# One core, attention into a gated convolution: a new hand-written order of 637 operations, with some query loads ahead of key and value loads

## The chip, the cores and the metric

One core of a Trainium2 chip runs the whole program. The metric is the device time of one execution in microseconds (us); the median over several runs of the same program is compared. The engines are TensorE (PE, with its weight loader PEld), VectorE (DVE), ScalarE (ACT), GpSimd (POOL) and SyncE (SP); POOL and SP do little here but issue DMA transfers.

## What is computed

A linear attention without softmax, normalised per head, feeds a feed-forward part with a convolution over the sequence and a gate:

```python
kv = einsum('bhsd,bhse->bhde', k, v)                # 8 batches, 8 heads, 576 rows, 64 wide
o = einsum('bhsd,bhde->bhse', q, kv)
o = o / sqrt(mean(o * o, axis=-1) + 1e-06) * g_norm
x = o.transpose(0, 2, 1, 3).reshape(8, 576, 512)
h = maximum(x @ w_in, 0)                            # 512 -> 1024
c = conv_w[0] * h[s-1] + conv_w[1] * h[s] + conv_w[2] * h[s+1]
out = (h * sigmoid(c)) @ w_out                      # 1024 -> 512
```

The inputs and the output are float32; the matrix products run in bfloat16 with float32 sums.

## The kernel before

The program is a list of 852 short tokens, the string `ORDER`. Each token names a small function, its arguments and, behind an `@`, the buffers that it takes; a loop at the end of the kernel calls the functions in the list's order. After that each instruction is tied to the one before it on its engine, so that the list alone sets the order of work on every engine; nothing is rescheduled. Semaphores hold an instruction back until its data and its buffer are there.

```python
for token in ORDER.split():
    what, _, at = token.partition("@")
    slots[:] = [int(s) for s in at.split(",")] if at else []
    name, *args = what.split(".")
    ops[name](*(int(a) if a.isdigit() else a for a in args))
```

The first argument of most tokens is the batch (0 to 7). Two batches share one buffer of `h` (a pair, 0 to 3), and there are two such buffers. PSUM is one tile `banks` of eight banks; `@2` means bank 2, or banks 2 and 3 where an operation takes two. The tokens that matter below, with the line under which the profile lists them:

- `Lq`, `Lk`, `Lv` (L347): POOL issues the load of q, k or v of one batch, with a cast to bfloat16. There are three buffers of q and two each of k and v, so a load waits until the last reader of the batch before it in the same buffer is through.
- `kv` (L402), `kz` (L479): k times v of a batch, 72 matmuls of 64 by 64 on quarters of the array. `kva` and `kvd` copy the result to `kvb` on ACT (L416) or DVE (L414). `kx` (L489, SP) copies `kvb` with its halves exchanged.
- `qt` (L433): transposes half of a batch's q on the PE; `qd` (L443, DVE) copies it out. Batches 6 and 7 use `tq` (L467, a transposing DMA on SP) instead.
- `ot` (L460), `ox` (L500): q times kv for a quarter of a batch, four matmuls on quarters of the array (64 by 64).
- Batches 2 and 3 are normalised in one way: `sq` (L509, ACT) squares, `on` (L528, PE) sums, `nl` (L545, ACT) takes the reciprocal root, `mo` (L556, DVE) writes the normalised `x`.
- Batches 4 to 7 go in pairs: `sq` and `oc` (L521, ACT, a copy), then `ss` (L566, PE, 16 matmuls on 32 columns), `ln` (L574, ACT), `sl` (L581 to L584, DVE, four steps), `sp` (L593, PE, two matmuls on 32 rows of the array that spread the factors), and `mu` (L599, DVE), which multiplies a quarter of `x`.
- `hk` (L658), `hs` (L628), `hm` (L613): `x @ w_in` for one of eight blocks `f` of 128 columns of `w_in`, over a half (`hk`, `hs`) or all (`hm`) of the rows of a batch. These use the full array. `hm` needs all four quarters of `x`. `rh` (L640) and `re` (L619) apply the maximum on ACT.
- The convolution and the gate are mostly on DVE: `ta` (L681, L682: two scaled copies), `aa` (L687), `ab` (L692), then `sg` (L698, sigmoid on ACT), then `mg` (L722, the product). They share two buffers `taps`.
- `om` (L732): four of the eight matmuls of `h @ w_out` for 128 rows of the output, on the full array; `ea` (L738, ACT) or `ed` (L743, DVE) copies the row block out of PSUM into one of six buffers `row`, and `st` (L748, SP) stores it. The last row block can be done in two halves of 256 columns: `oh` (L757), `eh` on ACT (L767) or `dh` on DVE (L772), `sh` (L777).

So the PE takes turns between three kinds of work: matmuls on the full array (`hk`, `hs`, `hm`, `on`, `om`), on quarters (`kv`, `kz`, `qt`, `ot`, `ox`), and on strips of 32 rows or columns (`sp`, `ss`). Below, a *run* is a stretch of PE work that is not on the full array, between two stretches that are.

Of the kernel before, what the change touches and what calls it, by code (L numbers as in the profile page):

```python
# [82 lines left out]
mo.2.0.1@2 om.0.3.0.4@4 ea.0.2@1 ot.2.1.1@6 ot.2.1.0@2 mg.1.1.0 om.0.3.4.4 ed.0.3@2 sq.2.1.0@1 sq.2.1.1@2 on.2.1.0@0
nl.2.1.0@9 mo.2.1.0 om.0.0.0.4@5 hk.1.3.0.0@4 on.2.1.1@0 st.0.2 nl.2.1.1@0 mo.2.1.1 om.0.0.4.4 ed.0.0@3 ot.2.0.0@2
sq.2.0.0@3 hk.1.3.0.1 rh.1.3.0 st.0.0 kv.3.0.2@0 kvd.3.0.2@0 on.2.0.0@6 nl.2.0.0@1 mo.2.0.0 hs.2.0.1@4 rh.2.0.1@1
hs.2.5.1@5 rh.2.5.1 ot.3.1.1@0 sq.3.1.1@4 ta.1.1.5@1 ot.3.0.1@6 sq.3.0.1@5 hs.2.1.1@4 rh.2.1.1 hs.2.4.0@5 rh.2.4.0
ta.1.1.4 ta.1.1.2@0 pn hs.2.4.1@2 rh.2.4.1 hs.2.1.0@3 rh.2.1.0 on.3.1.1@4 nl.3.1.1@2 hs.2.2.0@2 rh.2.2.0 hs.2.5.0@3
rh.2.5.0 on.3.0.1@4 nl.3.0.1@3 aa.1.1.2 mo.3.1.1@0 hs.2.2.1@2 rh.2.2.1 hs.2.0.0@3 rh.2.0.0 ot.3.0.0@0 sq.3.0.0@6
mo.3.0.1 qt.4.0.0@4 qd.4.0.0@3 ta.1.1.3 ab.1.1.2 aa.1.1.1 ot.3.1.0@2 sq.3.1.0@7 hs.2.3.1@6 rh.2.3.1 on.3.0.0@4
nl.3.0.0@4 hs.3.4.1@7 rh.3.4.1 hs.3.1.1@6 rh.3.1.1 on.3.1.0@4 nl.3.1.0@5 mo.3.0.0 hs.3.6.1@7 rh.3.6.1 hs.2.6.0@6  # L90
mo.3.1.0 qt.5.0.0@4 qd.5.0.0@0 ab.1.1.1 qt.4.1.0@0 qd.4.1.0@4 sg.1.1.5 sg.1.1.4 Lq.6.0.4@0 mg.1.1.2 ta.1.1.6@1
ta.1.1.7 aa.1.1.3 hs.2.3.0@7 rh.2.3.0 hs.3.0.1@2 rh.3.0.1 rh.2.6.0 sg.1.1.3 sg.1.1.2 hs.3.7.0@3 hs.3.2.0@4 rh.3.2.0
hs.3.3.0@5 rh.3.3.0 rh.3.7.0 kv.4.0.2@0 kvd.4.0.2@1 hs.3.0.0@2 hs.3.3.1@6 mg.1.1.1 Lk.5.0.4@0 rh.3.3.1 hs.3.2.1@7
rh.3.2.1 hs.3.7.1@4 rh.3.7.1 hs.3.6.0@5 rh.3.6.0 rh.3.0.0 ab.1.1.3 ta.2.2.2@0 ta.2.2.3 hs.3.4.0@3 rh.3.4.0 sg.1.1.7
hs.3.1.0@4 hs.3.5.0@5 sg.1.1.6 rh.3.1.0 qt.5.1.0@0 qd.5.1.0@2 ot.4.0.0@6 sq.4.0.0@0 mg.1.1.3 rh.3.5.0 om.0.7.0.4@2
Lv.5.0.4@1 Lq.7.0.4@1 Lk.6.0.4@1 oc.4.0.0@6 hs.2.7.1@3 rh.2.7.1 ot.4.0.1@0 sq.4.0.1@1 oc.4.0.1@7 kv.5.0.2@4 ta.2.2.0@1
kvd.5.0.2@2 ot.4.1.0@6 oc.4.1.0@8 om.0.7.4.4 aa.2.2.1 ta.2.2.1 ed.0.7@4 aa.2.2.0 ot.5.0.0@4 sq.4.1.0@2 sq.5.0.0@3
# [727 lines left out]
```

## Time and profile before

| | us |
|---|---|
| median of 3 runs (lowest to highest) | 177.68 (177.53 to 177.69) |
| span of the profiled execution, first to last instruction | 175.6 |
| PE busy | 167.9 |
| DVE busy | 149.5 |
| ACT busy | 148.9 |
| POOL busy | 22.2 |

The profiled execution's own time is not listed apart from its span; the median of the runs is 2.1 us above the span. "Busy" counts an instruction from its start to its end, so engines whose instructions overlap (PE above all) look busier than they are: on the PE the distance from one start to the next tells more than the length of a matmul. A releaser behind "<-" is what ended an idle stretch; "issue" means that the profile shows nothing that was waited for. The view by stretches has, for each engine, its busy time and in brackets its instructions, then the granted PE clock and the load on the DMA engines.

### The profile page before, as it was taken

How to read it: one execution, taken by the hardware profiler on the slowest of the kernel's cores; microseconds unless marked ns; L12 is line 12 of the kernel's file. 1: busy time of each engine (PE TensorE's matmuls, PEld its weight loads, DVE VectorE, ACT ScalarE, POOL GpSimd, SP SyncE). 2: the span in 40 equal slices, each digit the busy share in tenths (PEclk: the TensorE clock that was granted, in tenths of full speed). 3: DMA queues.
4: the chain of work that ended last, by engine and by line, in shares of the span. 5: the costliest groups of instructions: out<-in, count | busy, mean ns of one | idle time of the engine just before them, and what ended most of it. 6: DMA issues, size and time to landing. Idle time of an engine off the chain costs nothing.

```text
span 175.6 us, 5070 instructions
## 1 busy us (share of the span) xinstructions
PE 167.9 (96%) x2097; PEld 100.0 (57%) x2114; DVE 149.5 (85%) x290; ACT 148.9 (85%) x268; POOL 22.2 (13%) x35
## 2 busy tenths in 40 slices
PE   7979999999999999999999999999999999999992
PEld 2334766676447677644467764444877744444451
DVE  2796638899688899999999998989999999999950
ACT  2368899999978999999999998999999967676721
POOL 3094512200603013030000000000000000000000
PEclk9999999999999999999999999999999999999999
DMA  5999999999999999999999050330310003064486
GB/s 159 392 323 207 207 207 207 208 208 209 207 241 230 227 207 207 170 182 197 258 181 161 14 134 0 119 123 0 119 63 0 0 0 116 13 239 175 179 304 237
DMA packets 25911, 29.11 MB, mean 166 GB/s; under 512 B 6036, under 2 KB 20384, under 8 KB 25888
## 3 DMA queue, kind: packets, MB, share of 16 engines
q0 software_dynamic: 13296, 14.50, 49.2%
q1 hardware_dynamic: 12048, 13.11, 26.2%
q10 hardware_dynamic: 544, 1.18, 1.7%
q8 instruction: 16, 0.26, 0.6%
q14 instruction: 7, 0.06, 0.1%
HBM read 32.52 MB, written 9.44 MB: 239 GB/s over the span
## 4 chain that ended last, share of the span: by engine, by line
PE 76%; DVE 12%; ACT 5%; DMA 3%; issue 3%; ACTq 0%; DVEq 0%
PE banks L732 32%; PE banks L628 14%; PE banks L613 9%; PE banks L658 4%; DMA stg<-in_v_dram 3%; PE banks L460 3%; DVE h L722 2%; PE banks L708 2%; ACT taps L698 2%; PE banks L402 2%; PE banks L593 2%; PE banks L433 1%; PE banks L528 1%; DVE taps L681 1%; PE banks L286 1%
## 5 line engine op out<-in xcount | busy, mean ns | idle before, releaser
L732 PE MATMUL banks<-w_out_sb,h 128*128 128x512 bf16 x267 | 62.8, 379 | 1.2 <-issue 0.6
L698 ACT ACTIVATE taps<-taps,cw 128x576 bf16<-128x576 bf16 (+1 forms) x44 | 40.6, 958 | 5.7 <-DVE taps L692 5.5
L732 PEld LDWEIGHTS <-h 128*128 128x128 bf16 x280 | 26.2, 98 | 30.0 <-issue 1.1
L628 PE MATMUL banks<-x,w_in_sb 128*128 128x288 bf16 (+2 forms) x256 | 34.2, 286 | 0.0
L640 ACT ACTIVATE h<-banks 128x288 bf16<-128x288 f32 (+2 forms) x80 | 29.5, 460 | 0.3 <-PE banks L658 0.2
L628 PEld LDWEIGHTS <-w_in_sb 128*128 128x128 bf16 x256 | 24.4, 98 | 7.8 <-issue 0.8
L722 DVE TENSOR_TENSOR h<-h,taps 128x1152 bf16<-128x1152 bf16 (+1 forms) x24 | 22.8, 952 | 1.2 <-ACT taps L698 1.2
L687 DVE TENSOR_TENSOR taps<-taps 128x1152 bf16<-128x1152 bf16 (+1 forms) x22 | 21.5, 978 | 0.5
L509 ACT ACTIVATE sq<-banks 128x576 bf16<-128x576 f32 (+2 forms) x32 | 20.8, 691 | 1.1 <-PE banks L460 1.1
L692 DVE TENSOR_TENSOR taps<-taps,h 128x1152 bf16<-128x1152 bf16 (+1 forms) x22 | 21.4, 972 | 0.3
L681 DVE TENSOR_SCALAR taps<-h,cw 128x576 bf16<-128x576 bf16 (+1 forms) x44 | 18.7, 424 | 0.6 <-ACT h L665 0.5
L682 DVE TENSOR_SCALAR taps<-h,cw 128x576 bf16<-128x576 bf16 (+1 forms) x44 | 18.4, 418 | 0.0
L738 ACT ACTIVATE row<-banks 128x512 f32<-128x512 f32 x23 | 13.5, 597 | 5.7 <-PE banks L732 4.2
L658 PE MATMUL banks<-x,w_in_sb 128*128 128x288 bf16 (+2 forms) x128 | 17.7, 286 | 0.1
L613 PE MATMUL banks<-x,w_in_sb 128*128 128x288 bf16 x128 | 16.9, 286 | 0.0
L556 DVE SCALAR_TENSOR_TENSOR x<-banks,cw,rs 128x576 bf16<-128x576 f32 (+2 forms) x16 | 13.0, 816 | 3.9 <-ACT rs L545 3.6
L658 PEld LDWEIGHTS <-w_in_sb 128*128 128x128 bf16 x128 | 12.0, 98 | 4.4 <-issue 0.5
L227 ACT ACT_TABLE_LOAD x10 | 12.8, 1283 | 2.0 <-issue 1.8
L613 PEld LDWEIGHTS <-w_in_sb 128*128 128x128 bf16 x128 | 12.3, 98 | 3.7 <-issue 0.2
L443 DVE COPY qT<-banks 128x1152 bf16<-128x1152 bf16 (+2 forms) x13 | 8.8, 681 | 5.7 <-PE banks L433 5.7
L545 ACT ACTIVATE rs<-banks,eps_sb 128x576 f32<-128x576 f32 (+2 forms) x16 | 11.8, 740 | 1.1 <-PE banks L528 1.1
L599 DVE SCALAR_TENSOR_TENSOR x<-o,cw,banks 128x576 bf16<-128x576 f32 (+2 forms) x16 | 12.1, 810 | 0.7 <-PE banks L593 0.5
(89 smaller groups left out, 162.9 us busy)
## 6 DMA issues: line engine op xcount, KB each, us to landing
out_dram<-row SPq DMA_DIRECT2D x35, 256.0 KB, 2.3
q_sb<-in_q_dram POOLq DMA_DIRECT2D x6, 576.0 KB, 17.9
k_sb<-in_k_dram POOLq DMA_DIRECT2D x6, 576.0 KB, 14.5
v_sb<-in_v_dram POOLq DMA_DIRECT2D x6, 576.0 KB, 17.9
stg<-in_v_dram ACTq DMA_DIRECT2D x2, 576.0 KB, 6.2
stg<-in_k_dram SPq DMA_DIRECT2D x4, 288.0 KB, 6.9
w_in_sb<-in_moe_w_in_dram POOLq DMA_DIRECT2D x2, 512.0 KB, 9.9
w_out_sb<-in_moe_w_out_dram POOLq DMA_DIRECT2D x1, 1024.0 KB, 15.5
```

Source lines behind the costliest of these rows:

```text
L509: nc.scalar.activation(T["sq", b, u, s], T["o", b, u, s], AX.Square)
L613: nc.tensor.matmul(ps[:, s, :HS], w_in_sb[:, t, f * P:(f + 1) * P], T["x", b][:, t, c0:c1], start=(t == 0), stop=(t == NT - 1))
L628: nc.tensor.matmul(ps, w_in_sb[:, t, f * P:(f + 1) * P], T["x", b][:, t, c0:c1], start=(t == 0), stop=(t == NT - 1))
L640: nc.scalar.activation(h, fr, AX.Relu)
L658: nc.tensor.matmul(T[at], w_in_sb[:, t, f * P:(f + 1) * P], T["x", b][:, t, c0:c1], start=(t == 0), stop=(t == NT - 1))
L681: nc.vector.tensor_scalar_mul(tap[:, 0, f % 2, :n, 8:8 + S], h[:, f], cw[:, f:f + 1])
L682: nc.vector.tensor_scalar_mul(tap[:, 1, f % 2, :n, :S], h[:, f], cw[:, 2 * NF + f:2 * NF + f + 1])
L687: nc.vector.tensor_add(tap[:, 1, :, :n, :S], tap[:, 0, :, :n, 7:7 + S], tap[:, 1, :, :n, 1:1 + S])
L692: nc.vector.tensor_add(y, y, span(b, n)[:, 2 * j:2 * j + 2])
L698: nc.scalar.activation(y, y, AX.Sigmoid, scale=cw[:, NF + f:NF + f + 1])
L722: nc.vector.tensor_mul(h, h, tap_of(b, j)[:, 1, :, :n, :S])
L732: nc.tensor.matmul(T["om", p, m], h[:, f, m * P:(m + 1) * P], w_out_sb[:, f, :], start=(f == 0), stop=(f == NF - 1))
```

## The change

The first 215 tokens stay. The other 637 are put in another order, and many get other banks and buffers. No operation is added or taken away, except that 12 copies change their engine: `ed.0.0`, `ed.2.8`, `ed.3.0`, `ed.3.2`, `ed.3.7` and `kvd.3.0.2` move from DVE to ACT, `ea.0.2`, `ea.0.6`, `ea.3.1`, `ea.3.5` and the two half rows `eh.3.8.0` and `eh.3.8.1` from ACT to DVE. Of the diff, the lines where the lists part, a line of the middle, and the end:

```diff
-hk.1.7.0.0@0 mg.0.1.2 hk.1.7.1.0@1 hk.1.7.1.1 rh.1.7.1 hk.1.7.0.1 rh.1.7.0 ta.1.1.1@0 ta.1.1.0 Lk.2.0.4@1 Lv.2.0.4@0
-Lq.3.0.4@0 Lk.3.0.4@0 Lv.3.0.4@1 Lq.4.0.4@1 aa.1.1.0 hk.1.4.0.0@3 om.0.1.0.4@2 rh.1.4.1 hk.1.4.0.1 rh.1.4.0
...
-ed.3.7@4 om.3.5.4.4 ea.3.5@3 st.3.5 om.3.4.4.4 ed.3.4@5 st.3.4 st.3.7 om.3.6.4.4 ea.3.6@0 st.3.6 oh.3.8.1@1 eh.3.8.1@2
-sh.3.8.1 oh.3.8.0@0 eh.3.8.0@1 sh.3.8.0
+Lq.3.0.4@0 qt.3.1.0@0 rh.1.4.1 mg.0.1.2 ta.1.1.1@0 ta.1.1.0 aa.1.1.0 mg.0.1.3 hk.1.4.0.0@3 hk.1.4.0.1 hk.1.7.0.0@5
+hk.1.7.0.1 om.0.1.0.4@2 Lk.2.0.4@1 Lv.2.0.4@0 Lk.3.0.4@0 Lq.4.0.4@1 Lv.3.0.4@1 hk.1.7.1.0@6 ab.1.1.0 rh.1.7.0 rh.1.4.0
...
+mu.5.1.0 hm.5.1@2 re.4.0 ox.6.1.0@4 hm.4.4@6 re.4.6 hm.5.5@0 sq.6.1.0@1 re.4.4 oc.6.1.0@1 re.5.1 hm.5.7@6 re.5.5
...
+mg.7.1.2 om.3.5.4.4 ed.3.5@0 st.3.5 om.3.4.4.4 oh.3.8.1@0 ed.3.4@1 st.3.4 dh.3.8.1@2 oh.3.8.0@1 dh.3.8.0@3
+sh.3.8.1 sh.3.8.0 om.3.6.4.4 ea.3.6@0 st.3.6 om.3.7.4.4 ea.3.7@1 st.3.7
```

Counted in the two lists from the place where they part, the PE goes through 27 runs before and through 34 now, with the same 56 tokens in them; the work of the full array is the same too. What three places look like on the engines:

**The first loads on POOL** (k, v and q of whole batches, in the order of the queue). Before, from the load of q of batch 2 on:

```order
L347 DMA q_sb_727<-in_q_dram 128x4x576
L347 DMA k_sb_906<-in_k_dram 128x4x576
L347 DMA v_sb_908<-in_v_dram 128x4x576
L347 DMA q_sb_910<-in_q_dram 128x4x576
L347 DMA k_sb_912<-in_k_dram 128x4x576
L347 DMA v_sb_914<-in_v_dram 128x4x576
```

Now:

```order
L347 DMA q_sb_727<-in_q_dram 128x4x576
L347 DMA q_sb_891<-in_q_dram 128x4x576
L347 DMA k_sb_949<-in_k_dram 128x4x576
L347 DMA v_sb_951<-in_v_dram 128x4x576
L347 DMA k_sb_953<-in_k_dram 128x4x576
L347 DMA q_sb_955<-in_q_dram 128x4x576
L347 DMA v_sb_957<-in_v_dram 128x4x576
```

The load of q of batch 3 (the second row now) has moved ahead of k and v of batch 2, and q of batch 4 ahead of v of batch 3. Further down, q of batch 5 comes ahead of k and v of batch 4 in the same way, and v ahead of k for batches 5 to 7.

**DVE and PE where `x` of batches 4 and 5 is made and first used.** On DVE, before, the eight `mu` (L599) follow one another; the last three, and what comes behind them (`mg` and the first `ta`):

```order
L599 SCALAR_TENSOR_TENSOR x<-o_1921,cw,banks 128x2x288
L599 SCALAR_TENSOR_TENSOR x<-o_1861,cw,banks 128x2x288
L599 SCALAR_TENSOR_TENSOR x<-o_1838,cw,banks 128x2x288
L722 TENSOR_TENSOR h<-h,taps_72 128x2304
L681 TENSOR_SCALAR taps_72<-h,cw 128x2x576
L682 TENSOR_SCALAR taps_72<-h,cw 128x2x576
```

Now, from the fifth `mu` on:

```order
L599 SCALAR_TENSOR_TENSOR x<-o_1829,cw,banks 128x2x288
L743 COPY row<-banks 128x512
L599 SCALAR_TENSOR_TENSOR x<-o_1858,cw,banks 128x2x288
L722 TENSOR_TENSOR h<-h,taps_73 128x2304
L599 SCALAR_TENSOR_TENSOR x<-o_1881,cw,banks 128x2x288
L681 TENSOR_SCALAR taps_73<-h,cw 128x2x576
L682 TENSOR_SCALAR taps_73<-h,cw 128x2x576
L681 TENSOR_SCALAR taps_73<-h,cw 128x2x576
L682 TENSOR_SCALAR taps_73<-h,cw 128x2x576
L599 SCALAR_TENSOR_TENSOR x<-o_1929,cw,banks 128x2x288
```

A row copy, a product `mg` and four scaled copies now stand between the `mu`, and the eighth (`mu.5.1.0`) is behind all of them; a copy of `kvb` (L414) stands behind the first. On the PE, before, the last `sp` of batch 5 come in pairs behind an `hm` (the end of `hm.4.7`, two `sp`, the start of `hm.4.1`):

```order
L613 MATMUL banks<-x,w_in_sb 128x288
L593 LDWEIGHTS spread
L593 MATMUL banks<-wparts,spread 128x288
L593 LDWEIGHTS spread
L593 MATMUL banks<-wparts,spread 128x288
L593 LDWEIGHTS spread
L593 MATMUL banks<-wparts,spread 128x288
L593 LDWEIGHTS spread
L593 MATMUL banks<-wparts,spread 128x288
L613 LDWEIGHTS w_in_sb
```

Now the last one, `sp.5.1.0`, stands alone between `hm.4.6` and `hm.5.1`:

```order
L613 MATMUL banks<-x,w_in_sb 128x288
L593 LDWEIGHTS spread
L593 MATMUL banks<-wparts,spread 128x288
L593 LDWEIGHTS spread
L593 MATMUL banks<-wparts,spread 128x288
L613 LDWEIGHTS w_in_sb
```

The `hm.5.1` behind it reads the quarter of `x` that the eighth `mu` writes from this very `sp`, and takes the same two banks. Before, four `hm` of batch 4 stood between the last `sp` and `hm.5.1`.

**The end, on ACT.** Before, the last rows of ACT are three copies of whole rows and two of half rows:

```order
L698 ACTIVATE taps_73<-taps_73,cw 128x576 x2
L738 ACTIVATE row<-banks 128x512 x3
L767 ACTIVATE row<-banks 128x256 x2
```

Now:

```order
L698 ACTIVATE taps_72<-taps_72,cw 128x576 x2
L738 ACTIVATE row<-banks 128x512 x4
```

The half rows have gone to DVE (L772) and, on the PE, ahead of `om.3.6` and `om.3.7`; the last copy is now of a whole row.

More of the change, by code (lines that the diff above doesn't have):

```diff
@@ L83 @@
[L83 to L97, printed above, removed]
```

89 lines of the change are left out of this document (52 added, 37 removed).

## The prediction

> **What bounds the kernel now.** I read the page first (its first line), then the view by stretches, then the timeline of the PE.
>
> ```profile
> span 175.6 us, 5070 instructions
> ```
>
> ```profile
> 40.00:84.00 44.00, 43.33 (x799) 26.66 (x802) 39.84 (x73) 42.10 (x85) 8.15 (x11) 1.00 1.22 209
> 84.00:123.00 39.00, 38.37 (x416) 22.22 (x419) 36.67 (x51) 38.42 (x58) 0.00 (x0) 1.00 0.54 107
> 123.00:172.20 49.20, 49.03 (x297) 28.76 (x298) 45.40 (x80) 37.36 (x70) 0.00 (x0) 1.00 0.31 116
> ```
>
> The lists part at about 40 us, and the last matmul is at 172.2. In these 132.2 us (from left: the stretch, its length, then PE, PEld, DVE, ACT and POOL busy, the clock, the DMA share and GB/s) the PE is idle 0.67 + 0.63 + 0.17 = 1.5 us, always at the full clock. DVE and ACT are close behind (39.8 and 42.1 of 44 us, then 36.7 and 38.4 of 39), so an operation of theirs that comes late can stop the PE at once, but the path that sets the end is the PE's, instruction after instruction. A new order can win at most what the PE loses now: the 1.5 us of idle time, perhaps 1 us more that overlapping matmul records hide, and whatever it loses at the borders between kinds of matmul. These borders are in the timeline:
>
> ```profile
> 49.48 1.03 PE L732 MATMUL banks<-w_out_sb,h 128*128 128x512 bf16 x4
> 50.35 0.41 PE L658 MATMUL banks<-x,w_in_sb 128*128 128x288 bf16 x2
> ...
> 50.84 1.03 PE L732 MATMUL banks<-w_out_sb,h 128*128 128x512 bf16 x4
> 51.80 0.32 PE L460 MATMUL banks<-qT,kvb 64*64 64x288 bf16 x4
> 52.04 0.42 PE L658 MATMUL banks<-x,w_in_sb 128*128 128x288 bf16 x2
> ...
> 76.10 1.90 PE L732 MATMUL banks<-w_out_sb,h 128*128 128x512 bf16 x8
> 77.93 0.44 PE L460 MATMUL banks<-qT,kvb 64*64 64x288 bf16 x8
> 78.30 1.90 PE L732 MATMUL banks<-w_out_sb,h 128*128 128x512 bf16 x8
> 80.13 0.32 PE L460 MATMUL banks<-qT,kvb 64*64 64x288 bf16 x4
> 80.38 1.04 PE L732 MATMUL banks<-w_out_sb,h 128*128 128x512 bf16 x4
> ```
>
> ```profile
> PEld L460 <- issue: 2.4, 7, 0.4
> ```
>
> Four `om` matmuls take 50.35 - 49.48 = 0.87 us from start to start, 0.217 each. From 78.30 to 80.38 there are eight of them (1.74 us) and one `ot`: the `ot` costs 0.34 us (and 0.33 from 50.84 to 52.04). From 76.10 to 78.30 there are eight and two `ot`: 0.46 us. The second `ot` therefore costs 0.12 us, about the time that its 288 columns stream, and the other 0.22 us are paid once for each run, whatever is in it. The last row (the view of waits from 40 to 172.2 us: total, times, longest) is the same thing at the weight loader: it sits for 2.4 / 7 = 0.34 us before the first weights of such a run, waiting for nothing that the profile shows.
>
> **The change part by part.**
>
> *Runs.* The new list breaks the PE's small matmuls into 34 runs where there were 27; runs of a single token go from 6 to 17. The matmuls in them are the same. Seven runs at 0.22 us: **+1.55 us**, on the path, since the PE is what sets it. A gain is excluded, since no full matmul goes away. From above, the weight loader's 0.34 us for each would make 2.4. Three places in the rows give 0.22 from the PE's own starts, so I keep that.
>
> Of the Trainium skill, "TensorEngine Tiling (Array Packing)", section "Key Properties", says that a change of the tiling mode drains TensorE. By the 0.22 us above the trace agrees. "TensorE: Matmul & The Clock Gate", section "Single matmul latency", puts the part of a warm matmul's latency that does not grow with its columns at 166 ns; if each of the 14 further changes of mode cost that whole, an estimate from the page is 14 x 0.166 = 2.3 us and the sum below 0.8 us higher. The trace has the two borders of a run together at 0.22 us, and I go by the trace.
>
> *The place where `x` of batches 4 and 5 is made:* the PE's timeline, DVE's, and one of DVE's rows near the end for the length of a row copy.
>
> ```profile
> 81.35 0.67 PE L566 MATMUL banks<-sq,sel 128*32 128x288 bf16 x16
> ...
> 85.01 0.42 PE L593 MATMUL banks<-wparts,spread 32*128 32x288 bf16 x4
> ...
> 88.86 1.15 PE L613 MATMUL banks<-x,w_in_sb 128*128 128x288 bf16 x8
> 89.94 0.42 PE L593 MATMUL banks<-wparts,spread 32*128 32x288 bf16 x4
> 90.29 2.99 PE L613 MATMUL banks<-x,w_in_sb 128*128 128x288 bf16 x23
> ```
>
> ```profile
> 85.19 0.42 DVE L414 CAST kvb<-banks 128x256 bf16<-128x256 f32 x1 [0.24 <-PE banks L479]
> 85.53 6.29 DVE L599 SCALAR_TENSOR_TENSOR x<-o,cw,banks 128x576 bf16<-128x576 f32 x8
> 91.74 1.35 DVE L722 TENSOR_TENSOR h<-h,taps 128x2304 bf16<-128x2304 bf16 x1
> 93.00 0.52 DVE L681 TENSOR_SCALAR taps<-h,cw 128x1152 bf16<-128x1152 bf16 x1
> ...
> 94.84 1.36 DVE L687 TENSOR_TENSOR taps<-taps 128x2304 bf16<-128x2304 bf16 x1
> ```
>
> ```profile
> 166.57 2.00 DVE L743 COPY row<-banks 128x512 f32<-128x512 f32 x3
> ```
>
> Before, the eight `mu` run without a gap from 85.53 for 6.29 us, so the eighth is done at 91.82. `hm.5.1` comes four `hm` after 90.29; an `hm` is 8 matmuls and takes about 0.98 us (88.86 to 89.94 less 0.10 for the border), so it starts at 94.2, 2.4 us after its data. Now DVE has among the eight: the copy of `kvb` (85.19 to 85.53, 0.34), a row copy (2.00 / 3, 0.6 by its starts), the product `mg` (91.74 to 93.00, 1.26) and four scaled copies (93.00 to 94.84, 1.84). That makes 6.29 + 4.04 = 10.3 us from the first `mu` to the end of the eighth, and `hm.5.1` waits for it. The first `mu` can start some 0.4 us after the first `sp`, so `hm.5.1` starts no sooner than 10.7 us after the first `sp`; before it was 94.2 - 85.0 = 9.2. The first `sp` itself cannot be much sooner than now: from `ss` (81.35) to it (85.01) the chain over ACT and DVE takes 3.66 us, and the PE was filled with `om.0.6.0.4` and `kz` of batch 6, which the new order puts behind the first `sp`. So the PE stands for 1.5 us at these two spots, unless DVE gets ahead. The bounds: 0 if DVE comes to the place with enough work done early, 2.6 if it comes a `mg` (1.26) late and the chain slips. I take 1.2, below the sum, because some of the inserted work fills time in which DVE would have waited for an `sp`. Queued behind the eighth `mu` on DVE are `aa` and `mg` of pair 1, which `om` of this pair needs some 10 us later; they are not late.
>
> *The loads:* two issues on POOL, the two in the view of DMA issues (size and us from issue to landing), and the matmuls that use the first.
>
> ```profile
> 20.83 0.74 POOL L347 DMA_DIRECT2D v_sb<-in_v_dram  x1 [0.66 <-ACT h L665]
> 23.69 0.74 POOL L347 DMA_DIRECT2D q_sb<-in_q_dram  x1 [2.12 <-DVE sel L321]
> ```
>
> ```profile
> v_sb<-in_v_dram POOLq DMA_DIRECT2D x1, 576.0 KB, 20.1
> q_sb<-in_q_dram POOLq DMA_DIRECT2D x1, 576.0 KB, 20.1
> ```
>
> ```profile
> 43.17 0.78 PE L402 MATMUL banks<-v_sb,k_sb 64*64 64x64 bf16 x72
> ```
>
> v of batch 2 lands at 20.83 + 20.1 = 40.9, q of batch 3 at 43.8: POOL's queue delivers one after another, 2.9 us apart (the queue moves 209 GB/s in the first stretch above). Now v of batch 2 takes the later place, 43.8. `kv` of batch 2 starts at 43.17 before; the new order puts 1.1 us more of PE work ahead of it (the transposes of q of batch 3 in a run of their own, 0.5, and other `hk` for `om`), so it comes at 44.3, after the landing: 0, or 0.5 at worst. The other loads keep their place within one or two of the queue, and their users move with them; none is dropped or added.
>
> *The end:* the last row of ACT, the group of whole row copies (mean 597 ns), and the stores.
>
> ```profile
> 172.27 0.38 ACT L767 ACTIVATE row<-banks 128x256 f32<-128x256 f32 x1 [0.54 <-PE banks L757]
> ```
>
> ```profile
> L738 ACT ACTIVATE row<-banks 128x512 f32<-128x512 f32 x23 | 13.5, 597 | 5.7 <-PE banks L732 4.2 <-issue 1.4
> ```
>
> ```profile
> out_dram<-row SPq DMA_DIRECT2D x35, 256.0 KB, 2.3
> out_dram<-row SPq DMA_DIRECT2D x2, 128.0 KB, 2.2
> ```
>
> The last copy is of a whole row now: 0.60 instead of 0.38 us, and 256 KB instead of 128 KB to store, 0.1 us by the medians. These medians are of stores that share the DMA engines; the last one runs nearly alone, so the difference may be 0.3. **+0.4 us**, between 0.3 and 0.6, with nothing to cover it.
>
> *The copies that change engine* nearly cancel (ACT +0.60 for one more row and +0.4 for `kva.3`, less two halves at 0.38) and lie beside the PE's work: 0. If ACT had no cover, +0.3.
>
> *The other waits.* The PE's idle time of 1.5 us is spread over many small waits. A PE that comes later finds more of its data there; other short distances are new. I take -0.3, between -1.5 and +1.5.
>
> **Sum**, on the profiled span: 175.6 + 1.55 + 1.2 + 0 + 0.4 + 0 - 0.3 = 178.45. The median of the runs is 2.1 above the span: **180.5 us**, 1.6% slower.
>
> **The rivals.**
>
> *The new distances pay.* All of the PE's idle time goes, and the place of batches 4 and 5 is covered. Then 177.7 - 1.5 - 0.9 (hidden in the records) + 1.55 + 0.4 = 177.2. For it: many operations do have longer distances now. Against it: the eighth `mu` is the opposite, and the PE has hardly anything to give back. 5% for this end of it; another 7% that it comes out within a few tenths of 177.7.
>
> *DVE and ACT are the bound, not the PE.* They are busy for 90% and more up to 123 us; if the runs' 0.22 us only take the place of waits for them, the seven runs are free, and what is left is the 1.2 and the 0.4: 177.7 + 1.6 = 179.3. Against it: a single `ot` costs the same 0.33 to 0.34 us at 51 and at 80 us, and a wait for other engines would not come out alike. 20%.
>
> *The data come late in a row.* On SP, the transposing load of the second half of q of batch 6 now queues behind the copy of `kvb` and two row stores, while `ox.6.1.0`, which needs it, is two `hm` earlier on the PE; and `hm.5.1` is late by the 2.6. From the point where the load lands after the PE's arrival, each us is a us: another 2 us, 182.5. 15%.
>
> **How the numbers follow.** My forecast has 53%. The range from 178.5 to 182.4 leaves out the first rival and the far end of the last. What the measurement can tell from no change is about 0.2%, that is 177.3 to 178.0: faster than that 4%, within it 8%, slower 88%.
>
> **What would show it.** In the profile after, the timeline should have 34 runs, each single `ot` at 0.34 us between full matmuls. `hm.5.1` should start with a wait for L599, about 10.7 us after the first `sp`. The last matmul should be near 174.6, and the last ACT row a copy of 512 columns. I am wrong if the PE's busy stretches are not the ones that grow, if the eighth `mu` ends before `hm.5.1` is due, or if PE waits of a microsecond appear at places that I did not name.

## The result, and the profile after

| | before | after |
|---|---|---|
| median of the runs, us (lowest to highest) | 177.68 (177.53 to 177.69) | 182.81 (182.64 to 183.01) |
| span of the profiled execution, us | 175.6 | 181.2 |
| ratio after / before, 95% interval | | 1.0292 (1.0278 to 1.0307) |

The change makes the kernel 2.9% slower: 5.13 us by the medians, 5.6 us by the two profiled spans. The forecast was slower by 2.8 us (180.5), at most by 4.7 (182.4). The direction was right, the size was not.

The first view is the one by stretches: each line has the stretch, its length, then the busy time of PE, PEld, DVE, ACT and POOL with the number of instructions, the clock, the DMA share and GB/s. The cuts are now two marks on ACT, so that ACT does nearly the same work between them in both kernels: the start of `nl` of the quarter `ot.2.0.0` (batch 2), the start of the first `rh` of batch 7, and then the last matmul. Before:

```profile
40.00:53.56 13.56, 13.19 (x288) 7.58 (x289) 11.07 (x19) 11.79 (x23) 3.04 (x5) 1.00 1.19 224
53.56:124.12 70.56, 69.63 (x936) 42.19 (x942) 66.57 (x106) 69.85 (x122) 5.11 (x7) 1.00 0.83 146
124.12:172.20 48.08, 47.91 (x288) 27.88 (x289) 44.28 (x80) 36.24 (x69) 0.00 (x0) 1.00 0.32 118
```

The same stretches after:

```profile
40.00:54.48 14.48, 14.22 (x243) 7.42 (x245) 11.76 (x26) 12.60 (x25) 2.23 (x3) 1.00 1.21 208
54.48:128.40 73.92, 71.42 (x1008) 42.07 (x998) 66.42 (x100) 69.61 (x120) 5.34 (x7) 1.00 0.74 140
128.40:177.24 48.84, 48.70 (x294) 28.06 (x292) 44.27 (x80) 36.52 (x70) 0.00 (x0) 1.00 0.31 116
```

The 5.6 us are 0.9 up to the first mark, 3.4 between the marks, 0.8 up to the last matmul (172.2 and 177.24), and 0.6 behind it (175.6 - 172.2 = 3.4, now 181.2 - 177.24 = 4.0). Look at the middle line. ACT does 69.85 us of work in 70.56 before: it stands for 0.71 us, less than the PE (0.93). After, ACT has the same work (69.61 us) and stands for 4.31 us; the PE stands for 2.50. So ACT, which had been full, now waits for 3.6 us more in this stretch. What was waited for is in the view of waits for this stretch (what waited for what: total us, times, longest). ACT's waits before, and the only line of the PE:

```profile
ACT o L521 <- PE banks L500: 0.5, 1, 0.5
ACT rs L545 <- PE banks L528: 0.4, 1, 0.4
PE banks L732 <- issue: 0.5, 3, 0.2
```

The last line is not a wait. This trace holds 2097 matmul records to 2114 weight loads, and each of the three gaps of 0.16 us stands ahead of `om` matmuls of which there is one record less than weights loaded: a record is missing there. So 0.5 of the PE's 0.93 us before are no idle time.

ACT's waits after:

```profile
ACT sq L509 <- PE banks L500: 1.9, 1, 1.9
ACT h L619 <- PE banks L613: 1.0, 1, 1.0
ACT row L738 <- ACT o L521: 0.5, 1, 0.5
ACT h L619 <- DVE h L722: 0.3, 1, 0.3
```

And the PE, from 40 to 178 us, after:

```profile
PE banks L613 <- DVE x L599: 1.1, 1, 1.1
PE banks L593 <- DVE wparts L584: 0.4, 1, 0.4
PE banks L500 <- ACT row L738: 0.3, 1, 0.3
PE banks L433 <- ACT o L521: 0.3, 1, 0.3
PE banks L460 <- DVE kvb L414: 0.3, 1, 0.3
```

The first lines of the two lists after are one event. On the PE's timeline the wait in brackets stands ahead of `hm.5.1`; `ox.6.1.0` (L500) is right behind it, and the next ACT row begins when that is done:

```profile
86.37 0.30 PE L593 MATMUL banks<-wparts,spread 32*128 32x288 bf16 x4 [0.41 <-DVE wparts L584]
...
95.45 0.29 PE L593 MATMUL banks<-wparts,spread 32*128 32x288 bf16 x2
96.87 1.14 PE L613 MATMUL banks<-x,w_in_sb 128*128 128x288 bf16 x8 [1.12 <-DVE x L599]
97.94 0.33 PE L500 MATMUL banks<-qT,kvb 64*64 64x320 bf16 x4
```

```profile
98.38 0.70 ACT L509 ACTIVATE sq<-banks 128x640 bf16<-128x640 f32 x1 [1.90 <-PE banks L500]
```

DVE's timeline has the product (L722), and behind it the seventh `mu`, the scaled copies and the eighth `mu`:

```profile
92.12 1.35 DVE L722 TENSOR_TENSOR h<-h,taps 128x2304 bf16<-128x2304 bf16 x1
93.56 0.81 DVE L599 SCALAR_TENSOR_TENSOR x<-o,cw,banks 128x576 bf16<-128x576 f32 x1
...
96.01 0.81 DVE L599 SCALAR_TENSOR_TENSOR x<-o,cw,banks 128x576 bf16<-128x576 f32 x1
```

The last `mu` is held up behind them (it ends at 96.82), the PE for the `mu` (1.12), ACT for the PE (1.90). Behind this place DVE in its turn stands for a sigmoid of ACT, longer than anywhere else in the stretch; before, its longest such wait there was 0.67 us (at 106.50):

```profile
108.82 1.36 DVE L722 TENSOR_TENSOR h<-h,taps 128x2304 bf16<-128x2304 bf16 x1 [3.35 <-ACT taps L698]
```

So each engine passes a wait on to the next. How much of such a chain goes to the end, the lengths of the waits do not tell.

At the end, ACT's last two rows:

```profile
176.46 0.60 ACT L738 ACTIVATE row<-banks 128x512 f32<-128x512 f32 x1 [4.92 <-PE banks L732]
177.58 0.60 ACT L738 ACTIVATE row<-banks 128x512 f32<-128x512 f32 x1 [0.52 <-DMA out_dram<-row]
```

The last copy is of 512 columns, as foreseen, but it also waits 0.52 us for a store to free its row buffer.

### The profile page after: what moved, and what is told of

Same layout as the page of the kernel before. It is cut to its first block, busy times and chain, and to the rows that moved or that the text cites. A ratio compares the mean times of both kernels' runs of the same rounds, so it can differ in the third digit from the quotient of the medians.

```text
span 181.2 us, 5077 instructions
## 1 busy us (share of the span) xinstructions
PE 171.9 (95%) x2114; PEld 99.9 (55%) x2114; DVE 149.4 (82%) x290; ACT 149.6 (83%) x268; POOL 22.4 (12%) x35
## 4 chain that ended last, share of the span: by engine, by line
PE 40%; DVE 30%; ACT 17%; issue 6%; DMA 5%; SPq 0%; DVEq 0%; ACTq 0%
PE banks L732 11%; PE banks L658 7%; ACT taps L698 6%; DVE h L722 5%; DVE taps L692 5%; DVE taps L681 4%; DVE taps L682 4%; PE banks L628 4%; DVE taps L687 4%; PE banks L613 4%; DMA stg<-in_v_dram 3%; ACT h L619 3%; DMA out_dram<-row 3%; ACT row L738 2%; PE banks L286 2%
## 5 line engine op out<-in xcount | busy, mean ns | idle before, releaser
L732 PE MATMUL banks<-w_out_sb,h 128*128 128x512 bf16 x280 | 65.4, 379 | 0.2
L628 PE MATMUL banks<-x,w_in_sb 128*128 128x288 bf16 (+2 forms) x256 | 34.8, 286 | 0.0
L640 ACT ACTIVATE h<-banks 128x288 bf16<-128x288 f32 (+2 forms) x80 | 30.8, 451 | 0.6 <-PE banks L628 0.2
L628 PEld LDWEIGHTS <-w_in_sb 128*128 128x128 bf16 x256 | 24.1, 98 | 7.6 <-issue 0.2
L722 DVE TENSOR_TENSOR h<-h,taps 128x1152 bf16<-128x1152 bf16 (+1 forms) x24 | 22.8, 953 | 3.9 <-ACT taps L698 3.8
L681 DVE TENSOR_SCALAR taps<-h,cw 128x576 bf16<-128x576 bf16 (+1 forms) x44 | 19.0, 432 | 0.6 <-ACT h L665 0.5
L682 DVE TENSOR_SCALAR taps<-h,cw 128x576 bf16<-128x576 bf16 (+1 forms) x44 | 18.8, 428 | 0.0
L658 PE MATMUL banks<-x,w_in_sb 128*128 128x288 bf16 (+2 forms) x128 | 17.9, 286 | 0.0
L613 PEld LDWEIGHTS <-w_in_sb 128*128 128x128 bf16 x128 | 12.2, 98 | 5.6 <-issue 1.7
L443 DVE COPY qT<-banks 128x1152 bf16<-128x1152 bf16 (+2 forms) x13 | 8.8, 680 | 7.0 <-PE banks L433 7.0
L658 PEld LDWEIGHTS <-w_in_sb 128*128 128x128 bf16 x128 | 11.9, 98 | 4.2 <-issue 0.4
L599 DVE SCALAR_TENSOR_TENSOR x<-o,cw,banks 128x576 bf16<-128x576 f32 (+2 forms) x16 | 12.3, 809 | 1.7 <-PE banks L593 1.7
L286 PE MATMUL banks<-zero 128*128 128x512 bf16 x37 | 12.0, 450 | 1.2 <-DVE zero L265 1.2
```

Of the source, the lines that this page charges most:

```text
L613: nc.tensor.matmul(ps[:, s, :HS], w_in_sb[:, t, f * P:(f + 1) * P], T["x", b][:, t, c0:c1], start=(t == 0), stop=(t == NT - 1))
L628: nc.tensor.matmul(ps, w_in_sb[:, t, f * P:(f + 1) * P], T["x", b][:, t, c0:c1], start=(t == 0), stop=(t == NT - 1))
L640: nc.scalar.activation(h, fr, AX.Relu)
L658: nc.tensor.matmul(T[at], w_in_sb[:, t, f * P:(f + 1) * P], T["x", b][:, t, c0:c1], start=(t == 0), stop=(t == NT - 1))
L681: nc.vector.tensor_scalar_mul(tap[:, 0, f % 2, :n, 8:8 + S], h[:, f], cw[:, f:f + 1])
L682: nc.vector.tensor_scalar_mul(tap[:, 1, f % 2, :n, :S], h[:, f], cw[:, 2 * NF + f:2 * NF + f + 1])
```

## The experiments

All kernels are timed beside the kernel before, whose median was 177.7 or 177.8 each time. Edits are shown in the list's tokens.

**What a run costs.** An added token `dr` is one matmul on a quarter of the array, with eight columns, into a bank that the next full matmul opens; its result is not used. Fourteen of them stand in the list of the kernel before, each between two matmuls of the full array: in `d14late` from 123 to 163 us by its trace (the text below, written before, says 139 to 166), in `d14mid` from 54 to 76.

```diff
+    def dr():
+        ps = bank()
+        nc.tensor.matmul(ps[half(0), :8], zero[half(0), :D], zero[half(0), :8], start=True, stop=True)
...
-st.1.1 hs.7.6.0@6
+st.1.1 dr@6 hs.7.6.0@6
```

> The kernel before with 14 matmuls more between 139 and 166 us: each 64 rows by 64 columns, 8 columns wide, on a quarter of the array, into the bank that the next full matmul opens and overwrites. Each makes one more run. If a run costs 0.22 us on the path that sets the end, the median rises by 14 x 0.22 = 3.1 us to 180.8; if DVE and ACT are the bound in this stretch, by less than 0.5 us; if each of the two borders cost 0.166 us, by 4.6.

> The same 14 matmuls, now between 55 and 76 us, where ACT and DVE are over 90% busy. If the runs are on the path there too, +3.1 us (180.8). If they only take the place of waits for ACT and DVE, or if a PE that comes later finds its data there, +0 to +1.5. My theory says between 2.5 and 3.1, since the PE has few waits to give back here.

`d14late`: 180.78 us (180.71 to 180.84), ratio 1.0169 (1.0156 to 1.0182): 3.07 / 14 = 0.219 us each. `d14mid`: 181.24 (180.43 to 183.0), 1.0212 (1.0173 to 1.025): +3.5, of which its trace has one stall of 0.8 us by the PE's starts at another place (below, in brackets 0.61); without it 0.20 each, less surely, since its executions differ by 2.6 us. So a run costs 0.22 us on the PE, and nine tenths of that are paid even in the stretch where ACT and DVE are 90% busy and more. By the 166 ns that the Trainium skill gives for the fixed part of a matmul ("TensorE: Matmul & The Clock Gate", section "Single matmul latency"), two borders for each of the fourteen, an estimate is 4.6 us; the trace does not bear that out.

**The loads.** The kernel before, with its first loads in the new order and nothing else.

```diff
-Lk.2.0.4@1 Lv.2.0.4@0 Lq.3.0.4@0 Lk.3.0.4@0 Lv.3.0.4@1 Lq.4.0.4@1
+Lq.3.0.4@0 Lk.2.0.4@1 Lv.2.0.4@0 Lk.3.0.4@0 Lq.4.0.4@1 Lv.3.0.4@1
...
-Lk.4.0.4@1 Lv.4.0.4@0 Lq.5.0.4@2
+Lq.5.0.4@2 Lk.4.0.4@1 Lv.4.0.4@0
```

> The kernel before with the issues of three loads alone moved on POOL: q of batch 3 ahead of k and v of batch 2, q of batch 4 ahead of v of 3, q of batch 5 ahead of k and v of 4. kv of batch 2 then has its v some 2.9 us later than now, at about 43.8 us, against a start of 43.2. If the loads are no cause: 177.7 to 178.3. If they are the cause of a large part of the 5.1 us: above 179.5.

178.92 us (178.38 to 179.16), 1.0057 (1.0043 to 1.0072). Alone, it costs 1.2 us, more than "no cause" (178.3 at most) and less than "a large part" (above 179.5). Two rows of its PE timeline (its lines are numbered one lower):

```profile
44.05 0.77 PE L401 MATMUL banks<-v_sb,k_sb 64*64 64x64 bf16 x72 [0.73 <-DMA v_sb<-in_v_dram]
...
74.73 0.40 PE L627 MATMUL banks<-x,w_in_sb 128*128 128x288 bf16 x2 [0.39 <-issue]
```

`kv` of batch 2 now waits 0.73 us for its v. The second row is a stall inside one operation, with nothing that the profile shows (below). In the new list the same `kv` starts at 44.60, without a wait:

```profile
44.60 0.78 PE L402 MATMUL banks<-v_sb,k_sb 64*64 64x64 bf16 x72
```

That is 1.4 us later than in the kernel before (43.17) and half a microsecond behind the landing that `loads` shows. The new order of the loads costs the changed kernel nothing here, because its list has other PE work ahead of this `kv`.

**The place of batches 4 and 5.** `a_hm51` is the kernel after with the last two `mu`, and `hm.4.4` and `re.4.0` with them, put so that the product and the scaled copies come behind the eighth `mu`.

```diff
-re.4.1 mg.2.2.1 kx.6@0 Lv.7.0.4@1 Lk.7.0.4@0 st.0.8 st.0.3 mu.5.0.1 tq.6.1@0 sg.2.2.0 ta.2.2.4@1 ta.2.2.5 sp.5.1.0.4@2
-mu.5.1.0 hm.5.1@2 re.4.0 ox.6.1.0@4 hm.4.4@6 re.4.6
+re.4.1 mu.5.0.1 sp.5.1.0.4@2 mu.5.1.0 hm.4.4@6 mg.2.2.1 kx.6@0 Lv.7.0.4@1 Lk.7.0.4@0 st.0.8 st.0.3 tq.6.1@0 sg.2.2.0
+ta.2.2.4@1 ta.2.2.5 re.4.0 hm.5.1@2 ox.6.1.0@4 re.4.6
```

> The changed kernel with one place of the new list repaired: the seventh and eighth mu go ahead of mg and the four scaled copies on DVE, and hm.4.4 stands between the last sp and hm.5.1 on the PE. If the 1.18 us that hm.5.1 waits there are lost for the whole kernel: 182.8 - 1.2 = 181.6. If mg and the copies, now later, stop the PE elsewhere instead: 182.5 to 183.

182.17 us (182.1 to 182.33), 1.0244 (1.023 to 1.0258): 0.64 better than after, half of the forecast. `hm.5.1` starts without its wait. ACT's longest wait in the same stretch:

```profile
ACT sq L509 <- PE banks L500: 1.8, 1, 1.8
```

`sq.6.1.0` still waits 1.8 us, so ACT's wait is not only the PE's handed on. It needs `ox.6.1.0`, which stands on the PE behind a whole `hm` more than before the edit.

`a_act1` puts one ready operation (`re.4.4`) ahead of that waiting `sq.6.1.0` on ACT, on top of `a_hm51`; `a_act2` also puts two ahead of the `re.5.3` that waits for `hm.5.3`.

```diff
-hm.5.5@0 sq.6.1.0@1 re.4.4
+hm.5.5@0 re.4.4 sq.6.1.0@1
```

```diff
-mg.2.2.0 re.5.3 ab.2.2.2 ta.2.2.7@0 ta.2.2.6 aa.2.2.3 ab.2.2.3 oc.6.1.1@2 hm.5.0@4 sq.6.1.1@2
+mg.2.2.0 oc.6.1.1@2 sq.6.1.1@2 re.5.3 ab.2.2.2 ta.2.2.7@0 ta.2.2.6 aa.2.2.3 ab.2.2.3 hm.5.0@4
```

> The changed kernel with the repair at hm.5.1 and, on ACT, re.4.4 ahead of sq.6.1.0. In the repair at hm.5.1 alone ACT still stands 1.76 us for sq.6.1.0 with re.4.4 ready behind it, and the PE then waits 0.49 us for re.4.4. If ACT's idle time is what counts in this stretch: 182.2 - 1.3 = 180.9 (180.6 to 181.4). If the PE's waits alone count: 182.2 - 0.5 = 181.7. If the wait comes back elsewhere: 182.2.

> As the last one, with oc and sq of ox.6.1.1 ahead of re.5.3 on ACT as well, which stands 0.97 us there for the matmuls of hm.5.3. If ACT's idle time counts: 0.6 to 0.9 below the last one, near 180.1. If the PE's waits alone count, no change against the last one, since no PE wait is named there.

182.08 (182.07 to 182.23), 1.0246 (1.0232 to 1.0259), and 182.22 (182.0 to 182.83), 1.0255 (1.0237 to 1.0274): neither gains. In `a_act1` the waits on ACT are:

```profile
ACT h L619 <- PE banks L613: 1.4, 2, 1.0
ACT sq L509 <- PE banks L500: 0.7, 1, 0.7
ACT taps L698 <- DVE taps L692: 0.5, 1, 0.5
```

The 1.8 us have become 0.7, and next to nothing is won. `kz` of batch 7 starts 0.5 us sooner than in `a_hm51` (99.92 for 100.45). Some 11 us later, at the `ox` of batch 7, the PE loses this again, to two waits for ACT that `a_hm51` does not have:

```profile
110.90 0.33 PE L500 MATMUL banks<-qT,kvb 64*64 64x320 bf16 x4 [0.37 <-ACT h L619]
111.44 0.30 PE L500 MATMUL banks<-qT,kvx 64*64 64x256 bf16 x4 [0.21 <-ACT h L619]
```

DVE's waits had moved already in `a_hm51`. From 85 to 105 us DVE stands as long for the `sp` there as in `a_act1` (the first line is the same in both), and longer than in the kernel after (the second):

```profile
DVE x L599 <- PE banks L593: 3.3, 3, 1.5
```

```profile
DVE x L599 <- PE banks L593: 0.5, 1, 0.5
```

In the kernel after, the product and the scaled copies filled the time in which DVE would have stood for an `sp`. Taken out from between the `mu`, they leave it empty, and the 3.35 us for the sigmoid are gone in their place.

**Another wait of the PE, early.** In the kernel after, `qt.5.1.0` and `kv.5` stand in a run at 77 us with 0.3 us of waits. `a_kv5` has `aa` and `ta` of pair 2 behind them and behind the copy of `kvb` instead of ahead, and `ot.4.1.1` ahead of `qt.5.1.0`.

```diff
-ot.4.1.0@0 aa.2.2.1 ta.2.2.0@0 kv.5.0.2@2 qt.5.1.0@6 ed.0.7@0 ot.4.1.1@4 kvd.5.0.2@1
+ot.4.1.0@0 kv.5.0.2@2 ed.0.7@0 ot.4.1.1@4 qt.5.1.0@6 kvd.5.0.2@1 aa.2.2.1 ta.2.2.0@0
```

> The changed kernel with another place repaired: ot.4.1.1 ahead of the transposes of q of batch 5 (so that these no longer wait for the copy of ot.4.0.1 on ACT), and kvb of batch 5 copied ahead of aa and two scaled copies on DVE. The trace loses 0.78 us in this run. If a wait of this size counts in full: 182.8 - 0.7 = 182.1 (182.0 to 182.2). If what stands behind on DVE and ACT sets the time (the chain to the first sp at 86.4 us): 182.6 to 182.9.

184.31 us (184.13 to 184.43), 1.0363 (1.0349 to 1.0377): 1.5 slower than after. DVE's timeline there, and then the PE's:

```profile
75.70 0.69 DVE L743 COPY row<-banks 128x512 f32<-128x512 f32 x1 [1.20 <-PE banks L732]
76.74 0.42 DVE L414 CAST kvb<-banks 128x256 bf16<-128x256 f32 x1 [0.35 <-PE banks L402]
77.08 1.35 DVE L687 TENSOR_TENSOR taps<-taps 128x2304 bf16<-128x2304 bf16 x1
...
80.07 0.75 DVE L443 COPY qT<-banks 128x1152 bf16<-128x1152 bf16 x1
```

```profile
80.88 0.44 PE L460 MATMUL banks<-qT,kvb 64*64 64x288 bf16 x8 [1.29 <-DVE qT L443]
```

DVE now stands 1.20 + 0.35 = 1.55 us for the PE, with `aa` (1.35 us) behind it. `qd.5.1.0` (L443) starts at 80.07 where it started at 78.75, and the PE pays 1.29 us for it. So the edit made a wait: it put two copies that wait for the PE ahead of an `aa` that had been ready, and says little of whether the old wait could be had back.

**The end.** `a_tail` is the kernel after with the end of the kernel before: half rows last, on ACT, and no row buffer taken that a store still reads.

```diff
-om.3.4.4.4 oh.3.8.1@0 ed.3.4@1 st.3.4 dh.3.8.1@2 oh.3.8.0@1 dh.3.8.0@3
-sh.3.8.1 sh.3.8.0 om.3.6.4.4 ea.3.6@0 st.3.6 om.3.7.4.4 ea.3.7@1 st.3.7
+om.3.4.4.4 ed.3.4@5 st.3.4 om.3.6.4.4 ea.3.6@1 st.3.6 om.3.7.4.4 ed.3.7@2 st.3.7
+oh.3.8.1@0 eh.3.8.1@3 sh.3.8.1 oh.3.8.0@1 eh.3.8.0@4 sh.3.8.0
```

> The changed kernel with the old end: the two half rows last, copied by ACT, and no row buffer whose store is still under way. The last matmul to the end of the span should go from 4.0 back to 3.4 us: 182.8 - 0.55 = 182.3. If the wait for the row buffer alone was the loss: the same. If the end is covered by the stores before it: 182.8.

182.10 us (181.95 to 182.48), 1.0243 (1.0228 to 1.0259): 0.71 better than after. The new end costs that much.

**Several repairs at once.** `a_fix` joins `a_hm51`, `a_kv5`, `a_tail`, and puts `om.0.6.0.4`, `om.1.8.4.4` and `om.1.8.0.4` ahead of three more places where the PE waits. `a_moves` moves 12 single operations of the kernel after, each past a few others, towards the work that waits for it, and takes one run away. Among them:

```diff
-hm.5.1@2 re.4.0 ox.6.1.0@4 hm.4.4@6 re.4.6 hm.5.5@0 sq.6.1.0@1
+re.4.0 ox.6.1.0@4 hm.4.4@6 re.4.6 hm.5.5@0 sq.6.1.0@1 hm.5.1@2
...
-om.2.0.0.4@3 om.2.5.4.4
+om.2.5.4.4 om.2.0.0.4@3
```

> All three repairs, and three more moves: om.0.6.0.4 ahead of the first sp (0.49 us of wait), om.1.8.4.4 ahead of the three ox of batch 7 (0.40), om.1.8.0.4 ahead of hm.5.2 (0.30). The borders stay at 34. If the loss is borders plus waits at single places: 182.8 - 1.2 - 0.7 - 0.55 - 0.9 = 179.5 (179.2 to 180.0). If DVE and ACT have become the bound as a whole, so that a wait repaired here comes back there: above 181.

> The changed kernel with twelve operations moved by some places each in the list, on PE, ACT, DVE and SP, so that each in-order queue has work that is ready: on the PE hm.5.1 behind ox.6.1.0, hm.4.4 and hm.5.5, om.0.6.4.4 behind ox.6.0.0, and ox.7.0.1 behind its two neighbours; on ACT re.5.3 behind oc.6.1.1, sg.2.2.1 earlier; on DVE mg.7.1.1 ahead of aa.7.1.3; and six smaller ones. The 34 borders, the loads' order and the end stay. If the loss beyond borders and end sits in such single places, where an operation stands at the head of a queue before its data: 182.8 - 2.4 = 180.4 (180.0 to 181.2). If such waits come back elsewhere, as in the repairs before: 181.8 to 182.8.

`a_fix`: 183.46 us (183.41 to 183.53), 1.0317 (1.0303 to 1.0331), slower than after by 0.65. It holds two edits that gained 0.64 and 0.71 alone and `a_kv5`, which cost 1.50: together +0.15, so the three further moves and what the edits do to one another cost another 0.5. `a_moves`: 182.53 (182.31 to 182.98), 1.0278 (1.0264 to 1.0292), 0.28 better. Up to the last matmul it gains more than that: in the profiled executions the last eight `om` matmuls begin at 174.12, in the kernel after at 175.35, 1.2 us later. Behind them it loses 0.5 of this again (spans of 180.5 and 181.2). Its last row copy stands for a row buffer twice as long as after's:

```profile
176.88 0.60 ACT L738 ACTIVATE row<-banks 128x512 f32<-128x512 f32 x1 [1.05 <-DMA out_dram<-row]
```

**Is ACT full, or only busy?** Four copies of 128 by 512 in SBUF, with unused results, are added on ACT to the kernel before: in `x4mid` from 57 to 70 us, in `x4late` from 144 to 161.

```diff
+    def xa():
+        nc.scalar.activation(xout, xin, AX.Copy)
...
-hs.2.1.0@3 rh.2.1.0
+hs.2.1.0@3 xa rh.2.1.0
```

> The kernel before with four copies more on ACT (128x512 bf16 from SBUF to SBUF, some 0.6 us each by the row copies of 512 columns), in front of four rh between 56 and 70 us. Theory now: from 53 to 124 us ACT is as full as the PE (0.7 us idle of 70.6), so that time put on either one counts. Then the median rises by 4 x 0.6 = 2.4 us (2.0 to 2.6), to 180.1. Rival, which the prediction assumed for ACT's own work: the PE is the path and ACT lies beside it, +0 to +0.5.

> The same four copies in front of four sigmoids and row copies between 144 and 162 us, where ACT stands idle 1.1 to 1.7 us at each. Both theories: +0 to +0.3. It shows what the copies cost by themselves where ACT has room.

`x4mid`: 179.39 us (179.22 to 179.55), 1.009 (1.0078 to 1.0102): +1.67, 0.42 for each. `x4late`: 177.80 (177.57 to 178.51), 1.0006 (0.9995 to 1.0017): nothing. The group of the four in `x4mid` (ns: least, median, most; first and last start):

```profile
L297 ACT ACTIVATE xout<-xin x4: 619/629/662, 57.0 to 69.9; 128x512 f32<-128x512 bf16 x4
```

In `x4mid` each copy holds ACT for 0.52 us, from its start to the start of the next instruction (56.99 to 57.51 for the first), less than its length and less than the 0.6 expected. So from 57 to 70 us four fifths of added work on ACT go to the end of the kernel, and nine tenths of added work on the PE (`d14mid`); from 144 us on ACT has room, and from 123 us on the PE has not (`d14late`).

**Cutting the change in two by time.** Four kernels take the new list up to a place, and from there what is left in the old order: up to the first `ss` (`h_ss4`), to the first `sp` (`h_sp4`), to `hm.5.3` (`h_hm53`), to `om.2.1` (`h_om2`).

```diff
-the old list from hk.1.7.0.0 on
+the new list up to ss.4.4.2, then the operations that are left, in the old list's order
```

> The new list up to the first ss (83 us), then everything that is left in the order of the old list. The trace of the changed kernel is 1.6 us behind at this place, 0.3 of it from the start of the execution, 0.66 from three more runs and some 0.65 from waits. If the PE is the path and what it loses is never made up: 177.7 + 1.3 = 179.0. If later slack on the PE takes the delay up: within 0.3 us of 177.7. If the first stretch hides more than its own trace shows (later data for what follows): above 180.

> The new list up to its first sp (86 us), then everything that is left in the order of the old list. At this place the changed kernel is late by 1.35 us on ACT (ln at 82.58 for 81.23) and DVE, 0.3 of it from the start of the execution. If the order behind this place loses the rest: 177.7 + 1.2 = 178.9 (178.6 to 179.3). If the first part leaves the engines in a state that costs more later: above 180.

> The new list up to hm.5.3 (100 us), then the order of the old list. Between the first sp and here ACT stands 1.9 + 0.3 us for the matmuls that wait behind the late sp. If this place is the largest loss and it is not made up later: 178.9 + 2.2 = 181.1 (180.6 to 181.6). If the loss is spread over the places behind it: 179.5 to 180.3.

> The new list up to the first om of the third pair (144 us), then the order of the old list with its end. If all of the loss but the end's 0.7 us lies ahead of this place: 182.8 - 0.8 = 182.0. If the row copies of the last two pairs, moved between the engines, lose more: below 181.7.

182.52 us (181.86 to 182.64), 1.0259 (1.0244 to 1.0275); 183.12 (182.23 to 183.54), 1.0276 (1.0247 to 1.0305); 183.30 (183.27 to 183.48), 1.0304 (1.0282 to 1.0326); 189.97 (189.56 to 190.94), 1.0684 (1.0656 to 1.0712). The totals do not tell the parts apart: three of the joints make a wait of their own for a bank that the other list still holds. One line of the PE's waits of `h_sp4`, of `h_hm53` and of `h_om2`:

```profile
PE banks L479 <- ACT row L738: 2.0, 1, 2.0
PE banks L613 <- ACT sq L509: 1.7, 1, 1.7
PE banks L732 <- ACT row L738: 3.9, 1, 3.9
```

`h_ss4` has no such wait (its longest on the PE is 0.4 us), and its trace does tell something. Two marks on DVE are the first `mu` of batches 4 and 5 and the first of batches 6 and 7. The first mark is at 85.53 us before, at 86.79 after and at 88.16 in `h_ss4` (whose lines are numbered one lower); the second mark in this order:

```profile
118.61 4.35 DVE L599 SCALAR_TENSOR_TENSOR x<-o,cw,banks 128x512 bf16<-128x512 f32 x6 [0.45 <-PE banks L593]
123.30 4.30 DVE L599 SCALAR_TENSOR_TENSOR x<-o,cw,banks 128x512 bf16<-128x512 f32 x6 [0.94 <-PE banks L593]
121.55 4.34 DVE L598 SCALAR_TENSOR_TENSOR x<-o,cw,banks 128x512 bf16<-128x512 f32 x6 [0.45 <-PE banks L592]
```

Between the marks lie 33.1 us before, 36.5 after and 33.4 in `h_ss4`, which has the new list ahead of this stretch and the old one in it. So the old order adds next to nothing here, though it starts 2.6 us late, and the new order adds 3.4. Of these about 1.8 are work on the PE that the new list puts behind the first mark: `kz` of batch 6 (0.6) and two `om` (0.87 each) more, one `hs` (0.5) less, an estimate from the starts above. The other 1.6 are no more than the 1.12 us of `hm.5.1` and three further runs explain. `h_ss4` itself is late by its joint, ahead of the first mark, and by an ACT wait of 1.02 us for a row buffer at 130 us.

**A better old list?** `b_merge` takes two borders from the kernel before (`kv` of batch 3 and one `ot` of batch 1 join other runs); `b_moves` moves ten of its operations past their neighbours, on ACT and DVE mostly.

```diff
-oq.1.1.1@4 nl.1.1.1@6
+oq.1.1.1@4 ot.1.1.0@2 nl.1.1.1@6
...
-sq.2.0.0@3 hk.1.3.0.1 st.0.0 kv.3.0.2@0 kvd.3.0.2@0
+sq.2.0.0@3 kv.3.0.2@0 hk.1.3.0.1 st.0.0 kvd.3.0.2@0
```

```diff
-qt.4.1.0@0 qd.4.1.0@4 sg.1.1.5 sg.1.1.4 Lq.6.0.4@0 mg.1.1.2
+qt.4.1.0@0 sg.1.1.5 sg.1.1.4 Lq.6.0.4@0 mg.1.1.2 qd.4.1.0@4
```

> The kernel before with two borders less: kv of batch 3 joined to ot.2.0.0 (hk.1.3.0.1 behind it), and ot.1.1.0 joined to oq.1.1.1. Both lie before 54 us, where ACT stands idle at times and the PE sets the pace. If a border costs 0.22 us on the path: 177.7 - 0.44 = 177.3 (ratio 0.9975). If other engines set the pace there: 177.7.

> The kernel before with ten such moves, nine of them on DVE and ACT (among them mg.6.1.3 ahead of aa.7.1.0, mg.7.1.2 ahead of a row copy, ta.4.2.5 ahead of ta.4.2.7, aa.2.2.2 and ab.2.2.2 behind mg.2.2.0) and one on the PE (hs.3.0.0). Its three engines have some 1 to 3 us of idle time each between 54 and 124 us. If some of it can still be had: 177.7 - 0.6 = 177.1 (176.8 to 177.5). If the list has nothing left: 177.6 to 178.

183.59 us (181.46 to 184.99), 1.0286 (1.0241 to 1.0331), and 179.64 (179.33 to 179.99), 1.0111 (1.0097 to 1.0125): slower by 5.1 (177.8 times 0.0286) and 2.0, where a small gain was expected. The PE's waits of `b_merge`:

```profile
PE banks L479 <- DMA v_sb<-in_v_dram: 2.7, 1, 2.7
PE banks L658 <- DVE x L556: 1.1, 1, 1.1
```

The second line is the moved `ot`: its `mo` on DVE and the `hk` that need it come later. Then v of batch 6 lands at 89.0 us where it landed at 83.6, and the PE stands 2.7 us for it. Behind this wait the granted clock is 0.50 for 3.4 us (the last number but two):

```profile
89.53:92.94 3.41, 3.08 (x53) 1.03 (x41) 2.04 (x4) 0.51 (x2) 0.00 (x0) 0.50 0.84 183
```

So the loss is not that of the two moved tokens alone. In `b_moves` the PE stops at `kv` of batch 4, behind `qd.4.1.0`, and twice at `hs` whose banks ACT frees late. No version was found that beats the kernel before.

## Why the forecast was right in kind and too small

*The bound: "the path that sets the end is the PE's, instruction after instruction."* This is the sentence that failed, by half, and the term "the other waits" (below) failed with it. It holds from 123 us on: fourteen runs on the PE cost 0.219 us each there, and from 144 us on four copies on ACT nothing. Between 54 and 76 us it does not: there added work on either is paid for the greater part (`d14mid` 0.20 of 0.22, `x4mid` 0.42 of 0.52). Between 53.56 and 124.12 us before, PE, ACT and DVE stood for 0.93 (0.5 of it missing records), 0.71 and 3.99 us, so in the old list PE and ACT hand work to one another nearly without a gap, and DVE follows closely. That a wait of ACT for the PE is as dear there as one of the PE is argued from `x4mid`; no run takes such a wait away without making another. The "1.5 us of idle time" of the PE was read too high as well: five of its gaps, 0.8 us, are missing records.

*The runs.* 34 runs, +1.55 us: the term and its size hold, 0.219 us a run measured against 0.22 assumed. That is from runs added to the kernel before; the seven were not taken out of the kernel after. Its trace agrees: there are 34 runs, and from 77.75 to 78.95 us four `om` and one `ot` take 1.20 us, 0.33 more than the four `om` alone. The rival by which DVE and ACT are the bound and the runs are therefore free falls: ACT is a bound up to 124 us, but the runs were not free in `d14mid`.

*The place of batches 4 and 5.* The wait is where it was said, for what was said: `hm.5.1` starts 96.87 - 86.37 = 10.5 us after the first `sp` (10.7 forecast) with 1.12 us of waiting. With 0.41 at the first `sp` that is 1.5, where I wrote 1.2. What the term lacked is ACT's 1.90 us behind it. Undoing the place alone gives 0.64 us back; the rest came up elsewhere (DVE then stands for two `sp`).

*The loads.* Right at 0, and for the reason given: `kv` of batch 2 comes at 44.60 (44.3 forecast), behind its landing. `loads` shows the price where nothing is put ahead of it.

*The end.* 0.4 forecast, 0.7 measured (`a_tail`). The mechanism was right, but the 0.52 us wait of the last copy for its row buffer, written in the list by the buffer numbers, was missed.

*"The copies that change engine ... lie beside the PE's work: 0. If ACT had no cover, +0.3."* ACT has hardly any cover between 57 and 70 us (`x4mid`). What these copies cost was not measured alone.

*"The other waits: -0.3, between -1.5 and +1.5."* This is the term that was wrong. From 40 us to the end of the last matmul the PE takes 137.24 us where it took 132.2, 5.04 more. Without the 0.3 by which this execution was late already at 9 us, and without 1.55 for the seven runs, 3.2 are left. Of these 1.5 are at the named place and 1.7 at other places, some ten by the PE's starts, each of 0.2 to 0.8 (an estimate): +1.7 where -0.3 was forecast, just outside the bounds. The reason given, "a PE that comes later finds more of its data there", needs the other engines to run ahead of the PE. In the kernel after they don't: ACT stands 1.90 and 1.0 us for the PE, and DVE then 3.35 us for ACT. Of the signs named, the 34 runs, the wait of `hm.5.1` and the last row came; the last matmul ended at 177.24, not near 174.6. No PE wait of a microsecond came up at a place that was not named: the excess is in small ones.

The sum by the PE closes by its making, since the 3.2 are what was left: 1.55 (runs) + 3.2 (waits) + 0.6 (behind the last matmul) + 0.3 (already there at 9 us, in this one profiled execution) = 5.65, against 5.6 of span. Forecast was 1.55 + 1.2 - 0.3 + 0.4 = 2.85. The rival of late data (182.5) came nearest in size, but not by its mechanism: no load and no transposing transfer held the PE.

Measured alone, three parts of the 5.13 us are seen: the runs (7 x 0.219 = 1.5, by runs added to the kernel before), the end (0.7), the place of batches 4 and 5 (0.6). What is left, 2.3 us, is put down to many small waits. That they are a property of the order as a whole is argued from `a_act1` and `a_act2`, in which local repairs moved waits instead of removing them. It is not shown, and `a_moves` speaks against it in part: its twelve moves and one run less won 1.2 us up to the last matmuls. Not tried: `a_moves` with the old end, and all eight `mu` in one block in the new list.
